# Exact heads of the first batch: queries scaled and rounded in one ScalarE instruction, their remainder on VectorE

## The chip, the core and the metric

The kernel runs on one core of one Trainium2 chip. A core has five engines, each with its own queue that is worked off strictly in order: TensorE (PE in the profile; PEld is its weight load), VectorE (DVE), ScalarE (ACT), GpSimd (POOL) and SyncE (SP, which only issues DMA transfers here). Engines wait for each other through semaphores. The metric is the device time of one execution in microseconds; lower is better.

## What is computed

The reference runs an attention with a threshold and then two mixture-of-experts layers on its result:

```python
scores = scale * np.matmul(q, k.transpose(0, 1, 3, 2))      # 2 batches, 8 heads, 576 x 64, fp32
thresh = np.max(scores, axis=-1, keepdims=True) - tau
scores = np.where(scores >= thresh, scores, -1000000000.0)
attn = np.exp(scores - np.max(scores, axis=-1, keepdims=True))
attn = attn / (np.sum(attn, axis=-1, keepdims=True) + 1e-09)
out = np.matmul(attn, v)
...
for e in range(E):                                          # 8 experts, then 4 experts
    h = np.maximum(x @ w1[e], 0.0)
    out += P[:, e:e + 1] * (h @ w2[e])
```

The products need nearly fp32 accuracy. The kernel gets it mostly by splitting an operand into a high part (rounded to the type fp32r, which TensorE takes at full rate) and a low part (value minus high part), and summing the products of the parts.

## The kernel before

**Stages.** The first part of the program is the attention; the experts' weights are fetched and split beside it. From about 260 us on everything is matmuls of the experts.

**Units and steps.** Attention goes by units of 128 query rows of one head. The first batch's first 256 rows are the "exact" heads: eight heads, two units each, so unit u belongs to head u // 2, u = 0 to 15. Heads 0 and 1 use plain fp32 scores. Heads 2 to 7 use prepared queries and keys and are the ones touched here. The units after them (16 and on) belong to the remaining rows and the second batch.

`step` is called once per time step t and writes out, in a fixed order, the work of several units that are at different points of the pipeline. In words, in the order in which an engine meets it at step t:

- TensorE: the transposes of unit t-2 (`turn`, tiles `et`, `er`), the products with the values (`mix`, tile `pv`; two matmuls in one step and three in the next), the scores of unit t+2 (`scores`, tile `sc`, which has two buffers; before the change at L271).
- VectorE: the mask of unit t (L295: reads the scores and the exponentials `ex`, writes `ex`), the row maximum of unit t+1 (L276), two small instructions (the second, L281, is what the exponential of unit t+1 waits for), a reciprocal (L303), then whatever is queued as `later` (L366, the low part `xl` of an output), then the step's prepared work.
- ScalarE: copies of the transposes (L320, L322), in some steps the copy of an output (L365), the exponential of unit t+1 (L291), in even steps the rounding of a weight tile (`wh`, L96), then the step's prepared work.
- GpSimd: the normalisation of unit t (L305, in place on `ex`), in even steps the weight tile's low part (`wl`, L98), then the step's prepared work.

**Prepared work.** `plan` says at which step the keys and queries of a head are split. For head 2 the keys (`pk`) come at step 0 and the queries (`pq`) at step 1; for head 3 both at step 3, with the keys of head 4 behind them; the queries of heads 4, 5, 6 and 7 come at steps 4, 6, 8 and 10, the keys of heads 5, 6 and 7 at steps 5, 7 and 9. `pk` is one ScalarE cast (`kh`, L71) and one GpSimd subtraction (`kl`, L76). `pq` is described under the change. Queries hold the head's 64 dimensions twice, in partitions 0 to 63 and again in 64 to 127: after `pq` the upper half holds the low part, so that one matmul with the 128 partitions sums the two products.

**What holds what.** The scores of unit u+2 overwrite those of unit u: they start only when VectorE's mask of unit u is done. The mask of unit u waits for ScalarE's exponential of unit u; that one waits for VectorE's L281 of unit u, which comes behind the mask of unit u-1. So mask, maximum, L281 and exponential form a ring through VectorE and ScalarE that goes round once per unit. The tile written by L330 (`etl`) shares its memory with the exact heads' transposes and can be written only when TensorE has finished their last value product.

**DMA.** SyncE fetches keys, queries, values and weight tiles in a fixed order. The reload of a query buffer waits until the low part that reads it is done.

Of the kernel before, what the change touches and what calls it, by code (L numbers as in the profile page):

```python
# [11 lines left out]
AF = mybir.ActivationFunctionType  # L12
ALU = mybir.AluOpType
# [3 lines left out]
B, H, S, D = 2, 8, 576, 64  # L17
# [12 lines left out]
def attention_two_moe_kernel(ctx, tc, qP, kP, qT, kT, vp, tau, wg, w1, w1s, w2, dp, m2w1s, m2w2, out):  # L30
    nc = tc.nc
    V, A, G, T = nc.vector, nc.scalar, nc.gpsimd, nc.tensor

    def f(ap):
        return ap.bitcast(F32)
# [21 lines left out]
    esc = cp.tile([P, 1], F32, name="esc")  # L57
# [11 lines left out]
    def split(eh, el, hi, lo, src):  # L69
        if eh is A:  # L70
            A.copy(hi, src)  # L71
        elif eh is V:
            V.tensor_copy(hi, src)
        else:
            G.tensor_scalar(hi, src, 1.0, 1.0, op0=ALU.mult, op1=ALU.mult)
        el.tensor_tensor(lo, src, f(hi), op=ALU.subtract)  # L76
# [34 lines left out]
    class Attention:  # L111
# [117 lines left out]
        def prep(self, hd):  # L229
            pl = self.pl  # L230

            def pk():
                hd["kh"] = pl.tile([P, S], F32R, tag="kh", name="kh", bufs=2)
                hd["kl"] = pl.tile([P, S], F32R, tag="kl", name="kl", bufs=2)
                split(A, G, hd["kh"], hd["kl"], hd["k"])

            def pq():
                qs = hd["qs"] = pl.tile([P, hd["n"]], F32R, tag="qs", name="qs", bufs=2)
                A.activation(hd["q"], hd["q"], AF.Copy, scale=esc)
                A.copy(qs, hd["q"])  # L240
                G.tensor_tensor(qs[D:], hd["q"][D:], f(qs[D:]), op=ALU.subtract)
                if hd["rem"]:
                    c, z = hd["rem"]
                    G.tensor_scalar(hd["z"][:, z:z + D], f(qs[:, c:c + D]), 1.0, 1.0, op0=ALU.mult, op1=ALU.mult)
                self.lq -= 1

            def pv():
                hd["vs"] = pl.tile([P, 5, 2, D], F32R, tag="vhl", name="vhl", bufs=2)
                split(A, G, hd["vs"][:, :, 0, :], hd["vs"][:, :, 1, :], hd["v"])
                self.lv -= 1  # L250

            return (pk, pq) if hd["exact"] else (pk, pq, pv)
# [833 lines left out]
```

## Time and profile before

| quantity | value |
|---|---|
| median of 3 timed executions | 1343.94 us (1343.56 to 1344.52) |
| profiled execution, its own time | 1345.01 us |
| span of the profiled execution | 1343.2 us |
| TensorE busy | 1316.0 us (98%) |
| VectorE busy | 671.1 us (50%) |
| ScalarE busy | 566.6 us (42%) |
| GpSimd busy | 696.4 us (52%) |

The page's shares are means over the whole span. The change lies in the first 63 us, so what counts is read from views of that stretch: the busy time of each engine in it, the chain of waits that ended last (followed back from the last instruction), and the timeline of each engine, where a row gives the start, the duration, the engine, the line and the tile, and in brackets how long the engine stood idle before it and who ended that. One instruction can start a little before the one ahead of it on its engine has ended in the records, since they are pipelined. The profiled execution is 1.07 us above the median; differences are made in the profiled execution and then set on the median.

### The profile page before, as it was taken

To read this page: it belongs to the slowest core of one execution; us is meant where nothing else is said; L and a number is where in the kernel's file an instruction comes from. 1 tells how busy PE (TensorE), PEld (TensorE's weight loads), DVE (VectorE), ACT (ScalarE), POOL (GpSimd) and SP (SyncE) were. 2 spreads that over 40 slices of the span, in tenths; PEclk is the share of its full clock that TensorE was granted. 3 is DMA by queue.
4 is the path that set the end of the run, shared out by engine and by line. 5 is a ranking of instruction groups with operands and counts; after the bars stand their busy time and mean duration, and the time that the engine had idled before them with its cause. 6 is when DMAs were issued, how large, how long until landed. Compare 5 with 4: busy or idle time off the path is not lost.

```text
span 1343.2 us, 20906 instructions
## 1 busy us (share of the span) xinstructions
PE 1316.0 (98%) x7777; PEld 1164.1 (87%) x7777; DVE 671.1 (50%) x1526; ACT 566.6 (42%) x1300; POOL 696.4 (52%) x837
## 2 busy tenths in 40 slices
PE   7998999999999999999999999999899999999998
PEld 4597988899889899898988989888789898898987
DVE  5799988366853434343343433434334334343343
ACT  6887786333434333242332423235434233242321
POOL 6886975442866335434533543454963454354330
PEclk9999999999999999999999999999999999999999
DMA  4542330100321112011111201101101111120101
GB/s 150 161 127 69 102 97 17 32 24 25 103 71 42 46 43 61 24 56 48 35 52 41 63 25 56 48 25 55 48 24 56 48 33 49 46 63 24 32 9 63
DMA packets 42054, 73.58 MB, mean 55 GB/s; under 512 B 5088, under 2 KB 10336, under 8 KB 41952
## 3 DMA queue, kind: packets, MB, share of 16 engines
q1 hardware_dynamic: 41664, 71.96, 18.2%
q8 instruction: 61, 1.00, 0.3%
q14 instruction: 41, 0.34, 0.1%
q10 hardware_dynamic: 288, 0.28, 0.1%
HBM read 69.86 MB, written 2.36 MB: 54 GB/s over the span
## 4 chain that ended last, share of the span: by engine, by line
PE 86%; DVE 5%; ACT 3%; POOL 3%; issue 2%; DMA 1%; POOLq 0%; ACTq 0%; DVEq 0%
PE mm L1003 38%; PE mm L893 32%; PE mm L495 5%; PE mm L468 3%; PE sc L271 2%; PE pv L348 2%; DVE ex L295 1%; PE et L313 1%; DVE st L276 1%; ACT ex L291 1%; PE pv L357 1%; DVE etl L330 1%; POOL wl L76 1%; PE pv L355 1%; ACT eth L320 0%
## 5 line engine op out<-in xcount | busy, mean ns | idle before, releaser
L1003 PE MATMUL mm<-wh,hs 128*128 128x512 f32 x1344 | 435.4, 396 | 1.9 <-DVE hs L869 1.9
L76 POOL TENSOR_TENSOR wl<-raw,wh 128x512 fp32r<-128x512 f32 x154 | 199.1, 1305 | 337.5 <-ACT wh L71 335.5
L1003 PEld LDWEIGHTS mm<-wh,hs 128*128 128x128 f32 x1344 | 252.3, 188 | 64.1 <-DVE hs L869 8.4
L1011 DVE SCALAR_TENSOR_TENSOR acc<-mm,p,acc 128x512 f32<-128x512 f32 x181 | 135.8, 751 | 300.8 <-PE mm L1003 300.8
L1003 PE MATMUL mm<-wl,hs 128*128 128x512 f32 x672 | 264.2, 393 | 0.0
L898 ACT COPY s<-mm 128x288 f32<-128x288 f32 x84 | 33.6, 401 | 450.4 <-PE mm L893 450.4
L869 DVE SCALAR_TENSOR_TENSOR hs<-mm,hs 128x288 fp32r<-128x288 f32 x252 | 114.8, 456 | 103.5 <-ACT hs L868 103.0
L1003 PEld LDWEIGHTS mm<-wl,hs 128*128 128x128 f32 x672 | 126.6, 188 | 27.1
L893 PE MATMUL mm<-xh,wl 128*128 128x288 f32 x672 | 144.3, 296 | 2.5 <-ACT w L898 1.6
L893 PE MATMUL mm<-xl,wh 128*128 128x288 f32 x672 | 143.8, 295 | 0.0
L893 PE MATMUL mm<-xh,wh 128*128 128x288 f32 x672 | 143.8, 295 | 0.0
L76 POOL TENSOR_TENSOR wl<-ws,wh 128x512 fp32r<-128x512 f32 x88 | 115.8, 1319 | 36.4 <-ACT wh L71 26.7
L868 ACT ACTIVATE hs<-mm 128x288 fp32r<-128x288 f32 x252 | 104.2, 413 | 69.7 <-DVE mm L920 64.7
L893 PEld LDWEIGHTS mm<-xh,wl 128*128 128x128 f32 x672 | 110.1, 188 | 7.4 <-ACT w L898 2.3
L893 PEld LDWEIGHTS mm<-xh,wh 128*128 128x128 f32 x672 | 108.1, 188 | 0.0
L893 PE MATMUL mm<-xth,wl 128*128 128x288 f32 x504 | 108.0, 295 | 0.0
L893 PEld LDWEIGHTS mm<-xl,wh 128*128 128x128 f32 x672 | 107.9, 188 | 0.0
L893 PE MATMUL mm<-xth,wh 128*128 128x288 f32 x504 | 107.7, 295 | 0.0
L893 PE MATMUL mm<-xtl,wh 128*128 128x288 f32 x504 | 107.7, 295 | 0.0
L875 POOL TENSOR_SCALAR ht<-hs 128x128 fp32r<-128x128 f32 x168 | 49.7, 301 | 110.6 <-ACT hs L868 95.5
L71 ACT CAST wh<-raw 128x512 fp32r<-128x512 f32 x154 | 95.6, 623 | 14.5 <-PE mm L893 10.4
L631 POOL TENSOR_TENSOR ws<-raw 128x512 f32<-128x512 f32 x44 | 57.3, 1302 | 53.2 <-DMA raw<-in_w1s 31.9
(172 smaller groups left out, 2296.8 us busy)
## 6 DMA issues: line engine op xcount, KB each, us to landing
raw<-in_w SPq DMA_DIRECT2D x88, 256.0 KB, 3.0
raw<-in_w1s SPq DMA_DIRECT2D x56, 256.0 KB, 2.7
raw<-in_m2w1s SPq DMA_DIRECT2D x32, 256.0 KB, 2.7
raw<-in_m2w SPq DMA_DIRECT2D x32, 256.0 KB, 2.9
kr<-in_kT SPq DMA_DIRECT2D x22, 288.0 KB, 2.9
vr<-in_vp SPq DMA_DIRECT2D x24, 160.0 KB, 2.4
qr<-in_qT SPq DMA_DIRECT2D x8, 288.0 KB, 2.8
out_y<-acc SPq DMA_DIRECT2D x8, 256.0 KB, 2.0
```

The source lines that it names most:

```text
L71: A.copy(hi, src)
L76: el.tensor_tensor(lo, src, f(hi), op=ALU.subtract)
L468: T.matmul(ph[:, :n], lhsT=a[:, kt * P:(kt + 1) * P], rhs=x[:, kt, n0:n0 + n], start=i == 0 and kt == 0, stop=i == 2 and kt == KT - 1)
L495: T.matmul(py, lhsT=x, rhs=a, start=i == 0, stop=i == 3 * FT - 1)
L631: G.tensor_tensor(s, a, b, op=op)
L868: A.activation(hh, src, AF.Relu)
L869: V.scalar_tensor_tensor(hl, src, 0.0, f(hh), op0=ALU.max, op1=ALU.subtract)
L875: G.tensor_scalar(tail[j][:, :, q:q + 32], f(side[s][j][:, :, 2 * P:]), 1.0, 1.0, op0=ALU.mult, op1=ALU.mult)
L893: T.matmul(m, lhsT=w[:, (2 * g + kt) * P:(2 * g + kt + 1) * P], rhs=operand(u, kt, lo), start=first and j == 0, stop=j == len(ops) - 1, sk ...
L898: A.copy(z[name], m)
L1003: T.matmul(py, lhsT=hs[x][:, k, o:o + P], rhs=w, start=n == 0, stop=n == 3 * HF - 1)
L1011: V.scalar_tensor_tensor(acc[t], py, s, acc[t], op0=ALU.mult, op1=ALU.add)
```

## The change

`pq` of the exact heads that take the prepared path (heads 2 to 7, 256 columns each) is rewritten. Before, ScalarE scaled the queries in place (L239), ScalarE rounded them into `qs` (L240), and GpSimd subtracted on the upper 64 partitions (L241). Now ScalarE scales and rounds in one instruction, and VectorE computes query times scale minus the rounded value on the upper 64 partitions in one instruction with three inputs: the unscaled query, the scale `esc` (one number per partition) and the rounded `qs`. Other heads keep the old three instructions.

```diff
             def pq():
                 qs = hd["qs"] = pl.tile([P, hd["n"]], F32R, tag="qs", name="qs", bufs=2)
-                A.activation(hd["q"], hd["q"], AF.Copy, scale=esc)
-                A.copy(qs, hd["q"])
-                G.tensor_tensor(qs[D:], hd["q"][D:], f(qs[D:]), op=ALU.subtract)
+                if hd["exact"]:
+                    A.activation(qs, hd["q"], AF.Copy, scale=esc)
+                    V.scalar_tensor_tensor(qs[D:], hd["q"][D:], esc[D:], f(qs[D:]), op0=ALU.mult, op1=ALU.subtract)
+                else:
+                    A.activation(hd["q"], hd["q"], AF.Copy, scale=esc)
+                    A.copy(qs, hd["q"])
+                    G.tensor_tensor(qs[D:], hd["q"][D:], f(qs[D:]), op=ALU.subtract)
```

Line numbers behind these lines grow by four. Nothing else differs: TensorE's queue holds the same instructions in the same order, and SyncE's too (there the reloads of query buffers wait for VectorE where they waited for GpSimd).

VectorE's queue around the end of step 6 (head 5), from the maximum of one unit to the mask of the next; `ex,st<-sc,st,ex` is the mask. Before:

```order
L276 TENSOR_REDUCE st<-sc 128x1
L299 TENSOR_SCALAR st<-st 128x1
L281 TENSOR_SCALAR st<-st,on 128x1
L303 RECIPROCAL st<-st 128x1
L366 TENSOR_TENSOR xl<-pv,xh 64x256
L295 SCALAR_TENSOR_TENSOR ex,st<-sc,st,ex 128x576
```

The same place now:

```order
L280 TENSOR_REDUCE st<-sc 128x1
L303 TENSOR_SCALAR st<-st 128x1
L285 TENSOR_SCALAR st<-st,on 128x1
L307 RECIPROCAL st<-st 128x1
L370 TENSOR_TENSOR xl<-pv,xh 64x256
L241 SCALAR_TENSOR_TENSOR qs<-qr,esc,qs 64x256
L299 SCALAR_TENSOR_TENSOR ex,st<-sc,st,ex 128x576
```

The new instruction on `qs` stands ahead of the next unit's mask.

ScalarE's queue at the same step, from the exponential of one unit to that of the next (`wh` is the weight tile, `e_125` the transposes' copies). Before:

```order
L291 ACTIVATE ex<-sc,st 128x576
L96 CAST wh<-raw 128x512
L239 ACTIVATE qr<-qr,esc 128x256
L240 CAST qs<-qr 128x256
L320 COPY e_125<-et 128x4x128
L322 COPY e_125<-er 64x256
L291 ACTIVATE ex<-sc,st 128x576
```

Now:

```order
L295 ACTIVATE ex<-sc,st 128x576
L96 CAST wh<-raw 128x512
L240 ACTIVATE qs<-qr,esc 128x256
L324 COPY e_125<-et 128x4x128
L326 COPY e_125<-er 64x256
L295 ACTIVATE ex<-sc,st 128x576
```

One instruction between the weight tile and the copies is gone; the one left writes `qs` directly, behind the exponential and the weight tile as before.

GpSimd's queue at the same step (`wl` is the weight tile's low part, `ex<-ex,st` a normalisation). Before:

```order
L98 TENSOR_TENSOR wl<-raw,wh 128x512
L241 TENSOR_TENSOR qs<-qr,qs 64x256
L305 TENSOR_SCALAR ex<-ex,st 128x576
L76 TENSOR_TENSOR kl<-kr,kh 128x576
L305 TENSOR_SCALAR ex<-ex,st 128x576
```

Now:

```order
L98 TENSOR_TENSOR wl<-raw,wh 128x512
L309 TENSOR_SCALAR ex<-ex,st 128x576
L76 TENSOR_TENSOR kl<-kr,kh 128x576
L309 TENSOR_SCALAR ex<-ex,st 128x576
```

The subtraction on `qs` has left the place between the weight tile and the normalisation.

## Rows read from the trace of the kernel before

**Rows 1.** Busy time by stretch: us, busy (x instructions) of PE, PEld, DVE, ACT, POOL; PEclk.

```profile
22.00:63.00 41.00, 41.00 (x209) 25.06 (x210) 28.04 (x90) 34.81 (x71) 36.99 (x40) 0.96 0.58 167
63.00:260.00 197.00, 187.15 (x1275) 171.75 (x1276) 165.52 (x456) 143.22 (x283) 142.12 (x209) 1.00 0.26 76
```

**Rows 2.** Chain that ended last, in order of time: start us, us, what.

```profile
21.23 0.73 POOL qs L241
...
22.00 1.33 PE sc L271 x4
...
31.17 0.72 PE sc L271 x4
...
41.71 0.73 PE sc L271 x4
...
59.34 3.61 PE pv L348 x14
...
63.04 0.10 DVE etl L330
```

**Rows 3.** Timeline of ScalarE, step 6 to step 7.

```profile
28.62 0.74 ACT L291 ACTIVATE ex<-sc,st 128x576 f32<-128x576 f32 x1
29.25 0.61 ACT L96 CAST wh<-raw 128x512 fp32r<-128x512 f32 x1
29.76 0.51 ACT L239 ACTIVATE qr<-qr,esc 128x256 f32<-128x256 f32 x1
30.30 0.40 ACT L240 CAST qs<-qr 128x256 fp32r<-128x256 f32 x1
...
31.36 0.74 ACT L291 ACTIVATE ex<-sc,st 128x576 f32<-128x576 f32 x1
```

**Rows 4.** Timeline of VectorE: the mask of unit 4, then those of units 7 and 8.

```profile
19.13 0.82 DVE L295 SCALAR_TENSOR_TENSOR ex<-sc,st,ex 128x576 f32<-128x576 f32 x1 [1.05 <-ACT ex L291]
...
29.44 0.82 DVE L295 SCALAR_TENSOR_TENSOR ex<-sc,st,ex 128x576 f32<-128x576 f32 x1 [0.28 <-ACT ex L291]
...
30.97 0.21 DVE L281 TENSOR_SCALAR st<-st,on 128x1 f32<-128x1 f32 x1
...
32.13 0.82 DVE L295 SCALAR_TENSOR_TENSOR ex<-sc,st,ex 128x576 f32<-128x576 f32 x1 [0.87 <-ACT ex L291]
```

**Rows 5.** Timeline of GpSimd at step 6: the weight tile and the queries.

```profile
29.95 1.27 POOL L98 TENSOR_TENSOR wl<-raw,wh 128x512 fp32r<-128x512 f32 x1 [0.63 <-ACT wh L96]
31.29 0.74 POOL L241 TENSOR_TENSOR qs<-qr,qs 64x256 fp32r<-64x256 f32 x1
```

**Rows 6.** Instructions of L869 on VectorE, ns min/median/max: one from PSUM, one all-SBUF.

```profile
L869 DVE SCALAR_TENSOR_TENSOR hs<-mm,hs x252: 444/458/460, 333.7 to 1326.9; 128x288 fp32r<-128x288 f32 x126
...
L869 DVE SCALAR_TENSOR_TENSOR hs<-t,hs x84: 448/452/1265, 337.7 to 1325.3; 128x288 fp32r<-128x288 f32 x84
```

**Rows 7.** Timeline of VectorE in the expert stage, at 366 us.

```profile
366.40 1.12 DVE L869 SCALAR_TENSOR_TENSOR hs<-t,hs 128x288 fp32r<-128x288 f32 x1
367.45 0.45 DVE L869 SCALAR_TENSOR_TENSOR hs<-mm,hs 128x288 fp32r<-128x288 f32 x1
```

**Rows 8.** Timeline of GpSimd at the same time.

```profile
365.92 1.29 POOL L631 TENSOR_TENSOR ws<-raw,ws 128x512 f32<-128x512 f32 x1
```

**Rows 9.** Timeline of TensorE where it had stood idle for long.

```profile
22.00 0.85 PE L271 MATMUL sc<-kh,qs 128*128 128x288 f32 x2 [2.17 <-POOL qs L241]
...
25.83 0.53 PE L271 MATMUL sc<-kh,qs 128*128 128x288 f32 x2
...
124.80 0.63 PE L313 MATMUL et<-ident,ex 128*128 128x128 f32 x4 [1.35 <-DVE etl L330]
```

**Rows 10.** Busy time by stretch around such pauses (columns of rows 1; PEclk is third from last).

```profile
22.00:24.00 2.00, 2.00 (x9) 1.92 (x9) 1.46 (x3) 1.52 (x4) 1.97 (x2) 0.50 0.81 233
24.00:26.00 2.00, 2.00 (x7) 0.89 (x6) 0.71 (x5) 1.48 (x3) 1.92 (x3) 0.66 0.84 252
123.00:125.00 2.00, 0.65 (x6) 0.45 (x5) 1.57 (x6) 1.95 (x5) 1.43 (x2) 1.00 0.24 92
```

## Prediction

> **What bounds the kernel now.** I read the busy time by stretch first. The change lies between 13 and 50 us. From 22 to 63 us TensorE is busy for all of the 41.00 us, while VectorE has 28.04, ScalarE 34.81 and GpSimd 36.99 [rows 1]. Then the chain of waits: up to 22.00 it runs through GpSimd's low part of the queries, which the scores of unit 6 wait for, and from there to 63 us through TensorE alone [rows 2]. The scores of units 9 and 13 start at 31.17 and 41.71 [rows 2]: four units in 10.54, so 5.27 us per pair of units, one pair per head. At 63.04 VectorE's first `etl` follows the last value product (begun at 59.34) [rows 2]. What comes later starts from that product, so a delay of TensorE at 41.71 that isn't made good by 59 us goes to the end of the program: in 63 to 260 us no engine is saturated the whole time [rows 1], but every link of that chain starts from one before it, and I see no link with a fixed time that could absorb a shift.
>
> That TensorE is the bound says little about the margin. The ring through VectorE and ScalarE (mask, maximum, L281, exponential) is the next bound. From the timelines of step 6: the exponential starts at 28.62 and 0.82 later, at 29.44, the mask [rows 3, 4]. From the mask's start to the end of L281 it is 30.97 + 0.21 - 29.44 = 1.74, and the next exponential can start some 0.03 later (the mask at 32.13 follows the exponential's end, 31.36 + 0.74, by as much): 1.77. In the odd step the exponential starts at 31.36 and the mask at 32.13, 0.77 later [rows 3, 4]. Two rounds with 0.77 and 1.77 are 5.08, against 5.27 of TensorE: a margin of 0.19 per pair. VectorE's idle time ahead of masks (0.28 and 0.87 in rows 4) is not free; it is the wait for the exponential inside this ring.
>
> **The change part by part.** *ScalarE* loses one of two passes per head, 0.40 of 0.51 + 0.40 [rows 3]. Bounds for the pass that is left: 0.40 and 0.51; I take 0.51, since it scales as L239 does. The gain on the path is nothing: behind it stand copies that wait for TensorE. Six of them, 2.4 us, lie beside other work.
>
> *GpSimd* loses 0.74 per head [rows 5]. Only once was that on the path: at 21.23, right behind the keys' low part, with the scores of unit 6 at 22.00 [rows 2].
>
> *VectorE* gets six instructions on 64 partitions and 256 columns, and this is where the time goes. Each stands ahead of a mask and waits for ScalarE's `qs`, which in even steps comes behind the exponential **and** the weight tile: 29.76 + 0.51 = 30.27, that is 1.65 after the exponential started [rows 3]. The mask used to start 0.82 after it. So the new instruction is not done in VectorE's idle time; it holds up a mask that could have run, and with it the maximum, L281 and the next exponential queued behind.
>
> It also meets GpSimd. Its two tensor inputs, the query and `qs`, both lie in SBUF; between 22 and 63 us no VectorE instruction of the kernel before had that (mask, maximum and `xl` each read PSUM). The expert stage has both kinds in one line with one shape: with an input from PSUM L869 took 444 to 460 ns in all 252 cases, with both in SBUF 448 to 1265 [rows 6]. The long ones have a cause that can be seen: one started at 366.40 while GpSimd was in an instruction from 365.92 to 367.21, lasted 1.12, so to 367.52, 0.31 after GpSimd was done, and its successor started at 367.45, 0.24 after [rows 7, 8]. It waited for the running GpSimd instruction to end. In even steps that instruction will be the weight tile's low part: it starts at 29.95, ahead of the new one (ready at some 30.30), and ends at 31.22, 2.60 after the exponential [rows 5]. So the mask starts 2.60 + 0.24 = 2.84 after the exponential, where it was 0.82.
>
> The Trainium skill, "SBUF — State Buffer", section "Who interferes with whom", says that a VectorE instruction with two SBUF inputs contends with a GpSimd instruction that reads SBUF, and that the later one stands still until the first is through. By that rule, and by the all-SBUF rows, the sum is the +6.6 below; by the PSUM rows alone it would be the +2.4 of the second rival. The trace agrees: 1265 ns against 460 at most [rows 6].
>
> *The sum.* In step 3, GpSimd is in the keys' low part until about 21.2 (it took the queries at 21.23 [rows 2]), so the mask of unit 4 starts at 21.2 + 0.24 = 21.44, where it was 19.13 [rows 4]. The scores of unit 6 follow a mask's length (0.82, and 0.03 for the signal) later, 22.29 instead of 22.00. From there the ring: exponential of unit 5 at 21.44 + 1.77 = 23.21, mask 5 at + 2.84 = 26.05, exponential 6 at 27.82, mask 6 at + 0.77 = 28.59, exponential 7 at 30.36, where it was 28.62. A pair with a new instruction now takes 2.84 + 1.77 + 0.77 + 1.77 = 7.15 instead of 5.27, +1.88. After two more pairs exponential 11 starts at 44.66, mask 11, the last held up (head 7), at 47.50, and the scores of unit 13 at 48.35 instead of 41.71: **+6.6 us**. Behind that the ring without new instructions (5.08) is shorter than TensorE's pair again, so TensorE runs through and neither loses nor regains anything. The first of the six (step 1, head 2) delays a mask by 0.8, and its effect is overtaken by that of step 3. The profiled execution would go from 1345.01 to 1351.6; on the median, 1343.94 + 6.6 = **1350.5 us**. The DMA reloads of queries now wait for VectorE; they have a whole pair in hand.
>
> Unknown is how long the wait for GpSimd is each time: at least nothing (then 2.4), at most the whole of its longest instruction there, the keys' or weight tile's low part. I take 0.9, what the order of the two queues gives (31.22 less 30.30), since both starts hang on ScalarE's two neighbouring instructions and so keep their distance. If mask to next start is 0.1 more or less each time, the sum moves by about 0.5. So the forecast's own range is 1349.4 to 1351.6.
>
> **The rivals.** *The clock falls as well* (1352.2). Ahead of the scores of units 9, 11 and 13 TensorE will now stand idle for 7.15 - 5.27 = 1.9 us. A pause of 2.17 ended at 22.00 with the granted clock at 0.50 for the next 2 us and 0.66 for the 2 after that, about 3.4 us at 1.2 GHz; one of 1.35 at 124.80 left it at 1.00 [rows 9, 10]. 1.9 lies between. Such a stretch costs 1.7 us of TensorE work; behind the first two pauses the next pause absorbs it, behind the last nothing does: 1350.5 + 1.7. All three in full would be 1355.6.
>
> *The wait without the collision* (1346.3). The new instruction starts at 1.68 after the exponential, takes 0.42 to 0.45 (288 columns took 0.45 [rows 6]), and the mask starts at some 2.03: a pair of 6.34. The mask of unit 4 then starts at 20.45, exponential 7 at 28.56, exponential 11 at 41.24, the scores of unit 13 at 44.12: +2.4. Against it stand rows 6 and 7.
>
> *Hidden* (1343.9). TensorE remains the bound if the wait per pair stays below the margin of 0.19. Against it: `qs` is ready 0.83 after the mask could start.
>
> *Faster* (1341.5). GpSimd is rid of the queries, the scores of unit 6 come at 21.2, 0.8 earlier, and the shorter pause leaves the clock at 2.4 GHz: the stretch from 22.00 to 25.83 [rows 9], 3.83 at the low clock, takes about 2.27 (half of a pair less the third value product), 1.56 less. Together -2.4. The condition is that no mask is held up, that is, `qs` ready within 0.82 of the exponential's start; the queue order on ScalarE gives 1.65. The Trainium skill points this way: "GPSIMD Engine Reference", section "Engine selection", wants elementwise work on two inputs on VectorE, as GpSimd is about twice as slow there. The rows agree on the durations (0.74 against at most 0.45), but not that duration decides here: position in the queue does.
>
> **How the numbers follow.** Forecast 64%, clock 16%, no collision 10%, hidden 5%, faster 5%. Within 0.2% of 1343.94 (2.7 us, about what a measurement of this kernel can tell from no change) lie the hidden case, over half of the no-collision case and most of the faster one: 14%. Slower: 64 + 16 + 4 = 84%. Faster: 2%. The range reaches a little below the forecast's own, for collisions in some of the heads only, and up past the clock's 1352.2: 1348.4 to 1353.6.
>
> **What would show it.** In the profile after: L241 on VectorE six times at about 1.2 us instead of 0.45, those of the even steps ending 0.3 behind the weight tile's low part on GpSimd; masks ahead of which VectorE no longer idles for ScalarE's exponential but stands behind L241; scores of units 9, 11 and 13 waiting for the mask, with TensorE idle about 1.9 us ahead of each and pairs of about 7.15; from unit 13 on the old pace; everything past 63 us shifted by the same amount. L241 at 0.45 would prove the collision wrong; pairs of 5.27 the ring; a PEclk below 1.00 between 34 and 55 us would prove the clock rival right.

## The result

The changed kernel took 1352.37 us (median of 4 executions, 1352.16 to 1353.48) against 1343.75 us (4 executions, 1343.49 to 1344.52): slower, ratio 1.0059 with a 95% interval of 1.0046 to 1.0071. Its profiled execution took 1352.27 us, so 7.26 more than the 1345.01 of before's profile. The forecast was 1350.5 us, in a range of 1348.4 to 1353.6: the sign, the place and the mechanism were right, the size 1.9 us short; the section on why it came out so says where, and what in it was luck.

The page of the changed kernel: span, busy time by engine, and the shares of the chain that ended last.

```profile
span 1350.5 us, 20910 instructions
PE 1318.1 (98%) x7777; PEld 1164.4 (86%) x7777; DVE 677.2 (50%) x1532; ACT 565.1 (42%) x1294; POOL 693.6 (51%) x831
PE 85%; DVE 6%; ACT 4%; POOL 3%; issue 1%; DMA 0%; POOLq 0%; ACTq 0%; DVEq 0%
```

TensorE's share is 98% as before: the page doesn't show what happened. The stretch from 22 to 63 us does. Columns as in [rows 1].

```profile
22.00:63.00 41.00, 34.80 (x169) 20.59 (x170) 30.28 (x88) 28.36 (x57) 27.34 (x29) 0.92 0.45 132
63.00:260.00 197.00, 187.09 (x1275) 169.57 (x1275) 168.00 (x467) 147.62 (x291) 143.61 (x205) 1.00 0.27 79
```

TensorE, busy for all of the 41.00 us before [rows 1], is now busy for 34.80 of them and gets through 169 matmuls where it did 209. ScalarE and GpSimd are less busy too; only VectorE is busier. After 63 us the picture is that of before.

The chain of waits of the changed kernel, with start and duration, answers [rows 2]:

```profile
19.85 0.41 ACT qs L240
...
20.29 1.35 DVE qs L241
21.66 0.82 DVE ex L299 x2
...
27.04 1.33 PE sc L275 x4
...
33.05 1.21 DVE qs L241
34.28 0.83 DVE ex L299 x2
...
42.02 0.79 PE sc L275 x4
...
49.19 0.80 PE sc L275 x4
...
66.92 3.61 PE pv L352 x14
```

It ran through TensorE alone from 22 us on. Now it goes from the new VectorE instruction (L241) to the mask (L299) and on to the next L241, mostly through the ring, twice through TensorE (from 27.04, when its clock was low, and from 42.02), and leaves VectorE for good only at the scores of unit 13, 49.19.

The six new instructions (ns min/median/max, first and last start), and step 6 on ScalarE, GpSimd and VectorE, to be held against [rows 3 to 5]:

```profile
L241 DVE SCALAR_TENSOR_TENSOR qs<-qr,esc,qs x6: 533/1188/1336, 13.8 to 47.1; 64x256 fp32r<-64x256 f32 x6
...
31.36 0.74 ACT L295 ACTIVATE ex<-sc,st 128x576 f32<-128x576 f32 x1
32.00 0.62 ACT L96 CAST wh<-raw 128x512 fp32r<-128x512 f32 x1
32.51 0.51 ACT L240 ACTIVATE qs<-qr,esc 128x256 fp32r<-128x256 f32 x1
...
32.70 1.27 POOL L98 TENSOR_TENSOR wl<-raw,wh 128x512 fp32r<-128x512 f32 x1 [1.44 <-ACT wh L96]
...
33.05 1.20 DVE L241 SCALAR_TENSOR_TENSOR qs<-qr,esc,qs 64x256 fp32r<-64x256 f32 x1 [1.14 <-ACT qs L240]
34.28 0.82 DVE L299 SCALAR_TENSOR_TENSOR ex<-sc,st,ex 128x576 f32<-128x576 f32 x1
...
35.81 0.21 DVE L285 TENSOR_SCALAR st<-st,on 128x1 f32<-128x1 f32 x1
...
35.87 0.74 ACT L295 ACTIVATE ex<-sc,st 128x576 f32<-128x576 f32 x1 [2.12 <-DVE st L303]
```

VectorE idled 1.14 us for `qs`, started L241 at 33.05 beside GpSimd's weight tile (32.70 to 33.97), and ended at 34.25, 0.28 after it. The mask, ready when the exponential ended (32.10), started at 34.28; the next exponential, at 35.87, 1.59 later. It did not wait for L285, the L281 of before, which ran until 36.02: the exponential reads only the row maximum (its bias is `st[:, 0:1]`, written by L276 of before), so the ring's link is the row maximum, and not L281 as the section on what holds what and the prediction have it.

One thing the forecast's sum did not hold: a low clock of TensorE. Stretches of the changed kernel, PEclk third from last:

```profile
24.00:26.00 2.00, 2.00 (x5) 0.74 (x4) 1.06 (x1) 1.64 (x4) 1.58 (x2) 0.50 0.84 259
...
28.00:30.00 2.00, 2.00 (x9) 1.26 (x8) 1.48 (x4) 1.05 (x2) 1.61 (x2) 0.50 0.29 93
30.00:32.00 2.00, 2.00 (x9) 0.82 (x8) 0.76 (x5) 1.48 (x4) 1.25 (x2) 0.90 0.24 51
34.00:55.00 21.00, 16.48 (x88) 10.07 (x88) 16.49 (x48) 14.04 (x28) 12.56 (x13) 1.00 0.43 125
```

It is at 1.2 GHz from about 23.6 to 30.4 us, twice as long as in [rows 10], and at 2.4 GHz during all the later pauses.

### The profile page after: what moved, and what is told of

Read it like the earlier page. It is cut to its first block, busy times and chain, and to the rows that moved or that the text cites. A ratio compares the mean times of both kernels' runs of the same rounds, so it can differ in the third digit from the quotient of the medians.

```text
span 1350.5 us, 20910 instructions
## 1 busy us (share of the span) xinstructions
PE 1318.1 (98%) x7777; PEld 1164.4 (86%) x7777; DVE 677.2 (50%) x1532; ACT 565.1 (42%) x1294; POOL 693.6 (51%) x831
## 4 chain that ended last, share of the span: by engine, by line
PE 85%; DVE 6%; ACT 4%; POOL 3%; issue 1%; DMA 0%; POOLq 0%; ACTq 0%; DVEq 0%
PE mm L1007 38%; PE mm L897 33%; PE mm L499 5%; PE mm L472 3%; DVE ex L299 2%; PE sc L275 2%; DVE st L280 1%; PE et L317 1%; PE pv L352 1%; ACT ex L295 1%; DVE etl L334 1%; PE pv L361 1%; PE pv L359 1%; POOL wl L76 1%; DVE qs L241 0%
## 5 line engine op out<-in xcount | busy, mean ns | idle before, releaser
L1007 PEld LDWEIGHTS mm<-wl,hs 128*128 128x128 f32 x672 | 126.5, 188 | 27.2
```

Source lines behind the costliest of these rows:

```text
L1007: T.matmul(py, lhsT=hs[x][:, k, o:o + P], rhs=w, start=n == 0, stop=n == 3 * HF - 1)
```

## The experiments

Theory: the new instruction holds up the mask by its **place** (behind ScalarE's `qs`) and by a **collision** (it waits for GpSimd's running instruction when both its tensor inputs are in SBUF). Rivals: place alone; the **clock**; nothing but the shape of the instruction. The first four kernels ran together, beside 27 executions of the kernel before (median 1344.82); the next four too, beside 21 (median 1344.87).

### The low part left out

```diff
-                    V.scalar_tensor_tensor(qs[D:], hd["q"][D:], esc[D:], f(qs[D:]), op0=ALU.mult, op1=ALU.subtract)
```

> The changed kernel without its VectorE instruction: heads 2 to 7 keep ScalarE's one pass, and the low part of their queries is left out (the upper 64 partitions keep the rounded value). Theory A (the new VectorE instruction holds up the masks, by its place behind ScalarE and by a collision with GpSimd): all of the loss goes, TensorE is the bound again between 22 and 63 us, pairs of units of 5.27 us; the scores of unit 6 no longer wait for GpSimd's queries, up to 0.8 us earlier: 1341.5 to 1344. Rival B (the one-pass ScalarE instruction or the earlier GpSimd work disturbs something later): stays above 1347.

Measured: 1343.09 us (11 executions, 1341.62 to 1344.30), ratio 0.9984 (0.9975 to 0.9993). From 22 to 63 us:

```profile
22.00:63.00 41.00, 40.29 (x213) 24.32 (x212) 30.17 (x99) 35.14 (x70) 34.62 (x38) 1.00 0.57 174
```

TensorE is busy throughout again and pairs take 5.27. All of the loss is in that one instruction; what is left of the change gains 0.16% (0.07 to 0.25%).

### Two ScalarE passes kept, the subtraction alone on VectorE

```diff
-                    A.activation(qs, hd["q"], AF.Copy, scale=esc)
-                    V.scalar_tensor_tensor(qs[D:], hd["q"][D:], esc[D:], f(qs[D:]), op0=ALU.mult, op1=ALU.subtract)
+                    A.activation(hd["q"], hd["q"], AF.Copy, scale=esc)
+                    A.copy(qs, hd["q"])
+                    V.tensor_tensor(qs[D:], hd["q"][D:], f(qs[D:]), op=ALU.subtract)
```

> Half of the change: ScalarE does its two passes as before, only the subtraction goes to VectorE (two SBUF inputs). The rounded queries are ready 0.4 us later than in the changed kernel. Theory A with the collision: GpSimd's weight tile, which the VectorE instruction waits for, ends later than that anyway, so the mask starts no later: as the changed kernel, 1351.5 to 1353. Without a collision each of three or four masks would come 0.4 later: 1353.5 to 1354.5.

Measured: 1352.74 us (5 executions, 1351.38 to 1354.38), ratio 1.0064 (1.0051 to 1.0076). The first mask that is held up (head 2), then the exponential of unit 7, GpSimd's weight tile and VectorE in step 6 of this kernel:

```profile
14.88 0.82 DVE L300 SCALAR_TENSOR_TENSOR ex<-sc,st,ex 128x576 f32<-128x576 f32 x1
...
30.62 0.74 ACT L296 ACTIVATE ex<-sc,st 128x576 f32<-128x576 f32 x1
...
31.95 1.27 POOL L98 TENSOR_TENSOR wl<-raw,wh 128x512 fp32r<-128x512 f32 x1
...
32.74 0.76 DVE L242 TENSOR_TENSOR qs<-qr,qs 64x256 fp32r<-64x256 f32 x1 [1.53 <-ACT qs L241]
```

`qs` is ready 0.4 later, so the instruction starts later against the weight tile (0.79 after its start, in the changed kernel 0.35), and ends at 33.50, again 0.28 after the weight tile (33.22). The end of GpSimd's instruction sets it, not its own start or form. So from step 3 on the pass that the change saves on ScalarE is worth nothing. In step 1 it is worth something: with the exponential ahead of it at 12.50 (changed kernel: 12.49) the mask came at 14.88 instead of 14.32, 0.56 later, and the mask of unit 4 was late by as much (22.22 against 21.66). The equal times hide this, since the clock differed: here it was low only from about 23.8 to 27.2 us, the scores of unit 13 came at 48.44, and a second fall followed at 133 us.

### The second input from PSUM

```diff
-                    V.scalar_tensor_tensor(qs[D:], hd["q"][D:], esc[D:], f(qs[D:]), op0=ALU.mult, op1=ALU.subtract)
+                    sc = self.units[self.t + 1]["sc"][D:, 0, :hd["n"]]
+                    V.scalar_tensor_tensor(qs[D:], hd["q"][D:], esc[D:], sc, op0=ALU.mult, op1=ALU.subtract)
```

> The changed kernel with one operand replaced: the VectorE instruction subtracts a piece of the next unit's score tile, which lies in PSUM, instead of the rounded queries in SBUF (so the low part of heads 2 to 7 is a wrong value). Place, size and wait for ScalarE are the same (it waits for the same engine's instruction through the tile it overwrites). Theory A: no more than one SBUF input, so no wait for GpSimd, the instruction takes 0.42 to 0.45 us each time and only the wait for ScalarE is left: +2.4 to +3 on before, 1346 to 1347; pairs of 6.3 us. Rival: the collision is only how the record shows a wait for ScalarE, and the whole loss comes from the place: 1352.

Measured: 1347.26 us (11 executions, 1346.93 to 1348.74), ratio 1.0024 (1.0014 to 1.0033).

```profile
L242 DVE SCALAR_TENSOR_TENSOR qs<-qr,esc,sc x6: 486/488/489, 13.9 to 42.9; 64x256 fp32r<-64x256 f32 x6
...
29.93 1.28 POOL L98 TENSOR_TENSOR wl<-raw,wh 128x512 fp32r<-128x512 f32 x1
...
30.29 0.49 DVE L242 SCALAR_TENSOR_TENSOR qs<-qr,esc,sc 64x256 fp32r<-64x256 f32 x1 [1.09 <-ACT qs L240]
...
44.31 0.53 PE L276 MATMUL sc<-kh,qs 128*128 128x288 f32 x2 [1.12 <-DVE ex L300]
```

In the middle of the weight tile the same form takes 0.49 us, all six times. With one input from PSUM there is no collision; what remains is the place: pairs took 6.09 to 6.47, about the 6.3 expected, and the time lies 0.3 above the 1346 to 1347 expected. The Trainium skill, "SBUF — State Buffer", section "Who interferes with whom", makes the same distinction between inputs; the trace agrees, 488 against 1188 ns.

### The low part one step later

```diff
-                    V.scalar_tensor_tensor(qs[D:], hd["q"][D:], esc[D:], f(qs[D:]), op0=ALU.mult, op1=ALU.subtract)
+                    self.defer.append(lambda: V.scalar_tensor_tensor(qs[D:], hd["q"][D:], esc[D:], f(qs[D:]), op0=ALU.mult,
+                                                                     op1=ALU.subtract))
...
                 self.norm(d)
+            self.run(self.defer)
```

> The changed kernel with the VectorE instruction written out one step later, behind the next step's reciprocal (the scores that need it come later still). It then stands where VectorE idles 0.87 us for an exponential, its input is long done, and it starts ahead of GpSimd's normalisation. Theory A: no mask is held up by more than 0.1, TensorE is the bound again, the scores of unit 6 some 0.5 earlier than before: 1341.4 to 1344. Rival (the ring through VectorE and ScalarE has no room for six more instructions wherever they stand): pairs of 5.6 or more, 1345 to 1349.

Measured: 1343.27 us (11 executions, 1342.82 to 1344.82), ratio 0.9994 (0.9985 to 1.0003). L241 now stands behind the reciprocal, where VectorE has time and `qs` is long ready:

```profile
L241 DVE SCALAR_TENSOR_TENSOR qs<-qr,esc,qs x6: 484/487/1398, 15.6 to 40.5; 64x256 fp32r<-64x256 f32 x6
...
30.04 0.49 DVE L241 SCALAR_TENSOR_TENSOR qs<-qr,esc,qs 64x256 fp32r<-64x256 f32 x1
...
30.11 1.05 POOL L310 TENSOR_SCALAR ex<-ex,st 128x576 f32<-128x576 f32 x1
```

Here VectorE was first and GpSimd's normalisation, 0.74 otherwise, took 1.05 and ended 0.63 after it: the later one waits, whichever engine it is. The same work on the same engine costs nothing in this place. That rules the rival "shape of the instruction" out. Two things came out otherwise than expected. Head 4's instruction started behind the weight tile (24.40 against 24.23) and took the 1.40, yet pairs stayed at 5.27: the ring absorbed a wait of 0.9 once. And the scores of unit 6 waited for head 3's deferred instruction and came at 22.29, not 0.5 earlier.

### Queries ahead of the weight tile

The queries of heads 4 to 7 are issued ahead of the weight tile of their step:

```diff
-                for t, w in zip((k, q, v), self.prep(hd)):
-                    self.work.setdefault(t, []).append(w)
+                for i, (t, w) in enumerate(zip((k, q, v), self.prep(hd))):
+                    early = hd["exact"] and i == 1 and hd["h"] > 3
+                    (self.early if early else self.work).setdefault(t, []).append(w)
...
+            for w in self.early.pop(t, ()):
+                w()
             fill(0, bool(c and c["mix"]))
```

> The changed kernel with the queries of heads 4 to 7 issued ahead of the weight tile in their step: on ScalarE the queries' rounding comes right behind the exponential, and the weight tile's rounding, and with it GpSimd's low part of that tile, behind it. Theory (a VectorE instruction waits for a GpSimd instruction that runs already, so who comes first decides): L241 of heads 4 to 7 takes 0.45 to 0.5 us, its start is about 1.2 after the exponential's, mask at 1.7 to 2.1 after it, pairs 5.7 to 6.1 instead of 6.9 to 7.2, scores of unit 13 at 43 to 44, total 1344.6 to 1346.5 (1 to 2 us more if the clock falls behind the step-3 pause as before). Rival (any overlap of the two engines costs VectorE the same, whoever began): L241 stays near 1.2 us and the time near 1350.

Measured: 1347.64 us (9 executions, 1347.17 to 1350.70), ratio 1.0027 (1.0017 to 1.0036).

```profile
28.83 0.74 ACT L296 ACTIVATE ex<-sc,st 128x576 f32<-128x576 f32 x1
...
30.00 0.48 DVE L242 SCALAR_TENSOR_TENSOR qs<-qr,esc,qs 64x256 fp32r<-64x256 f32 x1 [0.89 <-ACT qs L241]
30.52 0.42 DVE L371 TENSOR_TENSOR xl<-pv,xh 64x256 fp32r<-64x256 f32 x1
30.56 1.27 POOL L98 TENSOR_TENSOR wl<-raw,wh 128x512 fp32r<-128x512 f32 x1 [0.51 <-ACT wh L96]
30.86 0.80 DVE L300 SCALAR_TENSOR_TENSOR ex<-sc,st,ex 128x576 f32<-128x576 f32 x1
```

With SBUF inputs and VectorE done before the weight tile starts (30.56), no collision: 0.48. (What an overlap costs when VectorE began is seen in the run before, not here.) The mask comes 2.03 after the exponential, at the upper end of the 1.7 to 2.1 expected, because `xl` (0.42), which used to run while VectorE waited, now stands behind it. Pairs took 5.91 to 6.28 and the scores of unit 13 came at 44.11, near the 44.31 of the PSUM run, though head 3's collision is left in (its instruction took 1.34 us at 20.28) and `qs` is ready earlier: order takes the collision of heads 4 to 7 away, most of the place's cost stays. The time expected, 1344.6 to 1346.5, was too low, for the same reason as the prediction's (below).

### Head 3's instruction alone left out

```diff
-                    V.scalar_tensor_tensor(qs[D:], hd["q"][D:], esc[D:], f(qs[D:]), op0=ALU.mult, op1=ALU.subtract)
+                    if hd["h"] != 3:
+                        V.scalar_tensor_tensor(qs[D:], hd["q"][D:], esc[D:], f(qs[D:]), op0=ALU.mult, op1=ALU.subtract)
```

> The changed kernel without the VectorE instruction of head 3 alone (that head's queries lack their low part; step 3), the other five stay. Theory (collisions add up one by one, and the clock's fall at 24 us in the changed kernel follows its pause ahead of the scores of unit 6): no pause ahead of unit 6, clock 1.00 from 22 to 32 us, mask of unit 4 at about 19.3, exponential of unit 7 near 27.7, pairs still 6.9 to 7.15 us, scores of unit 13 near 45.4, so about 1348.7 us: step 3 and the clock together then make some 3.6 of the changed kernel's extra time. Rival (TensorE has slack for a delay as early as step 3, only the last collisions count): as the changed kernel, 1352.4. Rival (the later pauses make the clock fall when the early one is gone): clock under 1.00 between 30 and 48 us, 1350 or more.

Measured: 1350.31 us (5 executions, 1348.84 to 1351.91), ratio 1.0042 (1.0030 to 1.0054). The scores of unit 13 started at 45.63 (expected 45.4), so head 3's instruction and the early fall of the clock are worth 49.19 - 45.63 = 3.56 (expected 3.6). The early pause and the early fall are gone. But another fall came behind the last pause, as the last of the expected readings had it:

```profile
46.00:48.00 2.00, 2.00 (x11) 1.38 (x9) 1.45 (x7) 1.30 (x2) 0.97 (x2) 0.56 0.75 255
48.00:50.00 2.00, 2.00 (x5) 0.57 (x4) 0.93 (x4) 0.92 (x2) 1.90 (x2) 0.50 0.07 26
...
45.63 0.85 PE sc L276 x4
...
66.41 3.61 PE pv L353 x14
```

From unit 13 to the last value products it took 20.78 instead of 17.73 (66.92 - 49.19 in the changed kernel): 3.1 us that nothing absorbs. The profiled execution took 1351.91; the one execution whose mean clock was 1.000 took 1348.84, against 1348.7 expected.

### The changed kernel again

> The changed kernel once more, on this chip beside the three others, to set their times against and to see how often TensorE's clock falls in it. Theory (the pause ahead of unit 6 makes the clock fall in nearly every execution, and each further fall costs about 1.4 us): 1352.2 to 1353.6, mean granted clock 0.997 or lower in nearly all executions; an execution with 0.999 or more would take 1350 to 1351. Rival (the clock makes no difference to the changed kernel, since its pauses absorb it): times the same whatever the mean clock.

Measured: 1351.78 us (6 executions, 1351.08 to 1354.79), ratio 1.0056 (1.0044 to 1.0068). Three executions had a mean clock of 0.999 and took 1351.08 to 1351.19; three had 0.997 and took 1352.37 to 1354.79. So the clock does count in it, but only half of the executions had 0.997, where nearly all were expected to, and none of the ten executions of this kernel seen here was free of a fall.

### The kernel before, three profiles more

> The kernel before, once more with a profile: its executions lie at about 1343.5 with a mean granted clock of 1.000, 1345.0 with 0.999 and 1346.5 with 0.997. Theory (one fall of TensorE's clock in the attention costs about 1.4 us and is all that sets them apart; the first profile, 1345.01, holds one at 22 us): a profile at clock 1.000 starts the scores of unit 13 near 40.2 and the last value products near 57.9 us, and takes 1343.5; one at 0.999 has 41.7 and 59.3, or a fall somewhere later. Rival (a fall this early is absorbed): the scores of unit 13 at 41.7 also without it.

> As the run before: the kernel before once more, since its clock differs from execution to execution. With a mean clock of 1.000 the last value products start near 57.9 us and the whole takes 1343.5; with 0.999 they start near 59.3, or later work holds the fall.

> As the two runs before: a third execution of the kernel before with its profile, for the same comparison of the start of the last value products (57.9 at clock 1.000, 59.3 at 0.999 with the fall at 22 us).

Measured: 1344.90 (mean clock 0.999; low from 22.5 to 26 us, scores of unit 13 at 41.80), 1344.89 (0.999; low at 126 to 129 us instead, scores of unit 13 at 40.22), and 1343.27 (1.000). The third, with its rows for TensorE, its stretch (columns as in [rows 10]) and the end of its chain:

```profile
22.03 0.53 PE L271 MATMUL sc<-kh,qs 128*128 128x288 f32 x2 [2.34 <-POOL qs L241]
24.31 0.53 PE L271 MATMUL sc<-kh,qs 128*128 128x288 f32 x2
...
22.00:24.00 2.00, 1.97 (x12) 1.54 (x13) 1.73 (x6) 1.97 (x6) 1.94 (x2) 1.00 0.82 212
...
40.20 0.73 PE sc L271 x4
...
57.83 2.37 PE pv L348 x9
```

Scores of unit 13 at 40.20, value products at 57.83; 40.2 and 57.9 were expected. The rival, that an early fall is absorbed, is wrong for this kernel: where TensorE is the bound, a fall goes to the end whole. The fall at 22 us in the first profile of before had cost 41.71 - 40.20 = 1.51 us, and [rows 9] (22.00 to 25.83) show where: here the same stretch takes 2.28.

### A mixture meant to beat both

Heads 4 to 7 one step later as above; head 2 as changed; head 3's queries ahead of its keys:

```diff
-                for t, w in zip((k, q, v), self.prep(hd)):
+                ws = list(zip((k, q, v), self.prep(hd)))
+                for t, w in ws[::-1] if hd["exact"] and hd["h"] == 3 else ws:
...
-                    V.scalar_tensor_tensor(qs[D:], hd["q"][D:], esc[D:], f(qs[D:]), op0=ALU.mult, op1=ALU.subtract)
+                    low = lambda: V.scalar_tensor_tensor(qs[D:], hd["q"][D:], esc[D:], f(qs[D:]), op0=ALU.mult, op1=ALU.subtract)
+                    self.defer.append(low) if hd["h"] > 3 else low()
...
                 self.norm(d)
+            self.run(self.defer)
```

> A version meant to be at least as fast as both: the low parts of heads 4 to 7 on VectorE, but run one step later behind the next unit's reciprocal; head 2 as in the changed kernel; head 3's queries issued ahead of its keys, so that its VectorE instruction is done before GpSimd's keys begin. Theory: no VectorE instruction waits for GpSimd (L241 at about 0.5 us each), scores of unit 6 at 20.5 to 21.3 and pairs of 5.27, no pause over 1.3 us ahead of unit 6, clock 1.00; 1342.0 to 1342.9, that is 0.05 to 0.1% under the kernel before. Rival (the exponential's ring takes the place of the collisions): pairs above 5.4 and no gain, 1343.5 to 1345.

Measured: 1344.34 us (11 executions, 1342.91 to 1344.66), ratio 0.9997 (0.9988 to 1.0005): no difference, and outside the 1342.0 to 1342.9 expected. The rival's time came out, but not what it rests on, pairs above 5.4. In the profiled execution (1343.00, clock 1.000) pairs took 5.27 as expected, but the scores of unit 6 came at 21.40 after a pause of 1.45, and one of the six instructions still took 0.74. Nine of the eleven executions had a mean clock of 0.998 or 0.999 and took 1344.07 to 1344.66; where it fell in those, no profile shows.

## Why the prediction came out as it did

**The accounting.** Where the clock is known, the delay of unit 13's scores against the undisturbed 40.20 is the delay of the whole program:

| kernel | scores of unit 13 | delay | execution | delay against 1343.27 |
|---|---|---|---|---|
| changed, profiled | 49.19 | 8.99 | 1352.27 | 9.00 |
| head 3's left out, clock 1.000 | 45.63 | 5.43 | 1348.84 | 5.57 |
| input from PSUM, clock 1.000 | 44.31 | 4.11 | 1346.96 to 1347.41 | 3.69 to 4.14 |
| queries first, clock 1.000 | 44.11 | 3.91 | 1347.17 | 3.90 |

(For the second and third row the start is that of their profiled execution, whose fall came after it; the time is that of other executions, without a fall.) Of the 8.99, the place makes 4.11, by the PSUM run. The clock makes about 1.25: the mask at 28.52 would have allowed exponential 7 at 30.11, 1.59 later, and it came at 31.36 behind copies that waited for slow value products. In the run with two passes, whose low clock ended at 27.2, that step took 1.53 (29.09 to 30.62). The rest, 3.6, is the collision, and the durations say the same: on the path the instruction took 1.34 us once and 1.19 to 1.20 four times, where the PSUM run has 0.49, together 3.7 more.

**Point by point.**

- *TensorE bounds, with 0.19 of margin per pair*: right that it bounds; pairs of 5.27 came back as soon as the instruction was gone or moved. The margin was larger: with 1.59 for 1.77 (below) two rounds are 4.72, so 0.55.
- *ScalarE's saved pass is worth nothing*: right from step 3 on, by the run with two passes, but for another reason than the one given: the copies behind it don't wait for TensorE in step 6 (the first started at 32.92, right behind `qs`); the mask waits for the weight tile either way. In step 1 the pass is worth 0.56, and that goes on at least to the mask of unit 6 (29.09 against 28.52). So step 3 doesn't overtake the effect of the first instruction, as the working has it: in the changed kernel the exponential of unit 4 came 0.19 later (18.55, before 18.36), about what mask 4 was late by.
- *Place, then collision, in even steps*: right in each of the four from step 4 on. Forecast were L241 at about 1.2 and an end 0.3 after the weight tile; the rows have 1.188 and 0.28.
- *Mask to next exponential 1.77*: too long, it is 1.59 in five of the seven rounds up to unit 13, 1.89 in one (41.14 to 43.03) and 2.84 in the one with the low clock. The exponential waits for the maximum and not for L281; the 1.77 of before held ScalarE's copies in it. That made the pairs 6.86 and 7.17 where 7.15 was forecast, and the pauses ahead of units 9, 11 and 13 were 1.25, 1.52 and 1.84 where 1.9 was.
- *The starts*: mask 4 forecast at 21.44, measured 21.66; scores of unit 6 at 22.29, 22.63; exponential 7 at 30.36, 31.36; mask 11 at 47.50, 48.31; scores of unit 13 at 48.35, 49.19. The shorter ring (0.9 in the five rounds) and the clock's 1.25, which the sum did not hold, nearly cancel: that these starts are off by no more than 1 us is in part luck.
- *What they were compared with*: **here the size went wrong.** +6.6 was taken against 41.71, a start that contained 1.51 us of low clock in before's own profile. The forecast chain, 48.35, held no such fall, so against a like execution it was 48.35 - 40.20 = 8.15. The working even names the 1.07 between that profile and the median and the 1.56 that the clock had cost there, but adds the 6.6 to the median as if the median held the fall as well. That median, 1343.94, lies among the executions without a fall: of the 48 beside the experiments 19 had a mean clock of 1.000 and took 1343.13 to 1344.08, 22 had 0.998 or 0.999 and took 1344.67 to 1345.54, 7 had 0.997 and took 1346.21 to 1346.63. The absolute end, 1351.6 for the profiled execution, was 0.7 short; the one set on the median 1.9.
- *No loss or gain after unit 13*: right; 17.73 to the last value products against 17.63 in the undisturbed execution, and the end shifted by as much.
- *The clock rival*: wrong about the place in this kernel, since the clock stayed at 1.00 through the pauses ahead of units 9, 11 and 13, and right that falls come behind such pauses: one came early, and with head 3's instruction gone one came behind the last pause, and cost 3.1 us where 1.7 was reckoned. Its basis, the length of the pause, doesn't hold (last section).
- *The wait without the collision*, reckoned at unit 13 in 44.12: the run built for it has 44.31, again with a late start (mask 4 at 20.91, reckoned at 20.45) and a short ring that nearly cancel. *Hidden* and *faster*: excluded; *faster* had about the right size for its condition, since without the instruction unit 13 started at 38.85: 2.86 before the 41.71, where 2.4 was reckoned, and 1.35 before the undisturbed 40.20.

## What to carry to other kernels

Before moving an instruction to an engine with spare time, look at what stands behind it in that engine's queue and at when its operands are ready: the same 0.49 us, without any collision, cost 4.1 us in all ahead of a mask that could have run, and nothing one step later. A VectorE instruction with two SBUF inputs and a GpSimd instruction that reads SBUF held each other up here, the one that came later waiting (0.7 to 0.9 us on VectorE, 0.3 on GpSimd), so issue first the one that work is waiting behind, or feed it from PSUM. And check that the profile from which a difference is taken is itself undisturbed: a clock fall of 3.4 us in the reference, worth 1.5, was the largest error here.

## What the runs showed of the hardware

- The length of a pause didn't decide whether the clock fell. In the kernel before a pause of 2.17 was followed by a fall [rows 9, 10], one of 2.34 in the same place was not; in the changed kernel one of 1.82 was followed by one that lasted 6.8 us, and the pauses of 1.25, 1.52 and 1.84 were not, though with head 3's instruction gone the pause of 1.84 ahead of unit 13 was:

```profile
22.63 0.50 PE L275 MATMUL sc<-kh,qs 128*128 128x288 f32 x2 [1.82 <-DVE ex L299]
...
35.16 0.53 PE L275 MATMUL sc<-kh,qs 128*128 128x288 f32 x2 [1.25 <-DVE ex L299]
...
42.02 0.52 PE L275 MATMUL sc<-kh,qs 128*128 128x288 f32 x2 [1.52 <-DVE ex L299]
...
49.19 0.53 PE L275 MATMUL sc<-kh,qs 128*128 128x288 f32 x2 [1.84 <-DVE ex L299]
```

- It also fell where TensorE had not paused: in the profile without the low part at 271.6 us, in the expert stage, with TensorE busy for all of the 2 us before (up to 270.1 with 18 products of only 8 columns each). What decides it stays open.
- A fall of 3.4 us cost 1.5 to 1.6 us in the kernel before where TensorE is the bound; one of 6.8 us cost 3.1 behind unit 13, where TensorE is the bound too, and about 1.25 where the ring had slack. The executions of the kernel before lie in steps of about 1.5 us by their mean clock, which fits none, one and two such falls.
